# One more half of a gated convolution taken as weighted sums out of PSUM: a memory attention kernel whose order of work is written out as a list

## The chip, the cores and the metric

The kernel runs on one core of a Trainium2 chip. The metric is the device time of one execution in microseconds (us). The engines of the core work from queues of their own, each strictly in the order in which the program gave it instructions: TensorE (PE in the profile, its weight loads PEld) for matrix products, VectorE (DVE), ScalarE (ACT), GpSimd (POOL), and SyncE (SP), which here only issues DMA transfers. An engine waits at the head of its queue until what its next instruction reads has been written, and until the buffer it writes has been given up.

## What is computed

The inputs are `q`, `k`, `v` (8 batches x 8 heads x 576 positions x 64), `phi` (8 x 8 x 576 x 32), a projection `w_val` and `w_out` (512 x 512 each) and `conv_w` (5 x 512). Cut to what matters:

```python
a = exp(phi - max over s);  a = a / sum over s            # per batch, head, slot
k_m, v_m = a.T @ k, a.T @ v                               # 32 slots x 64 per head
p = softmax(q @ k_m.T / 8)                                # s x 32 per head
x = p @ v_m                                               # heads side by side: s x 512
gate = sigmoid(sum over i of conv_w[i] * x shifted by i)  # causal, five taps, per channel
out = (gate * (x @ w_val)) @ w_out
```

## The kernel before, in words

All eight batches run through the same steps. A batch's 576 positions are cut into two **halves** `s` = 0, 1 of 288 columns, and its 512 channels into two **groups** `g` = 0, 1 of four heads each. Values are laid out with channels (or slots) on the 128 partitions and positions along the free axis.

For a batch `b`: `load_phi`, `phi_max`, `phi_turn`, `phi_top`, `phi_spread`, `phi_lay`, `phi_sub`, `phi_exp` make the unnormalised slot weights; `slots` (L397) multiplies them with `k` and `v`; `slots_inv` and `slots_scale` (L404, L406, L416/L418) normalise; `slots_turn` and `slots_place` transpose the result; `scores` (L447) is the product with `q`, in PSUM tiles called `cv`; `scores_turn` (L459), `soft_max`, `soft_sub` (L492), `soft_exp`, `soft_sum`, `soft_inv`, `soft_mul` (L519) and `soft_turn` (L525) are the softmax, whose last step writes the tile `pT` (probabilities, slots on partitions). Each batch needs its `pT` before the two ways to the gate can start.

The pre-activation of the gate is made in one of two ways, half by half:

- `conv(b, s)` (L585): `taps` has multiplied `v_m` with each of the five tap weights; TensorE then accumulates five shifted products per head, 40 matrix products for a half, and `sigmoid` (L632) reads the finished sum from PSUM.
- `mix(b, s)` (L598): 8 matrix products make `x` itself for 292 columns, in PSUM. Then `tap(b, s, g, i)` adds the five taps: i = 0 is a scaled copy on ACT (L620), i = 1 to 4 are multiply-adds on DVE (L622), each of two planes of 288 columns. If the step is marked with a star, tap 4 goes by ACT into a tile `part` of its own and POOL adds it (L614). `open_gate` (L627) is the sigmoid.

`cv` has two PSUM buffers, which `scores`, `conv` and `mix` share; each is given up when the last reader of it is done. Then `value` (L642, six products of two-piece operands, for a quarter of the channels) makes `x @ w_val`; `gated` (L655) multiplies by the gate, on DVE, or after a copy by ACT (L653) on POOL; `gated_high` and `gated_low` (L214, L217) split the product into two pieces; `project` (L675) is 12 products with `w_out`; `place` copies the result to SBUF, `store` writes it out. `value`, `project`, `slots` and all transposes share four PSUM buffers called `b`. At the start the three weights are also converted from 64-bit floating point by `narrow_size` and `narrow_round` on ACT (L273, L286), `narrow_bits` on DVE (L278), `narrow_add` on POOL (L292) and `narrow_done` on DVE (L301). `warm` is a few products whose result nobody reads.

What sets the order is one text, `ORDER`: a list of about 950 step names. A loop at the end of the kernel runs it from front to back, and each step appends its instructions to the queues of its engines. A star at a name makes the step take its other engine (`pick(usual, other)`). So the list fixes the order on each engine's queue and on SP's. In the kernel before, both halves of batch 0 go by `conv` and the other 14 halves by `mix`.

Of the kernel before, what the change touches and what calls it, by code (L numbers as in the profile page):

```python
# [43 lines left out]
warm.8 phi_exp.0.0 narrow_round.v.2 place_taps.0 narrow_bits.v.2 narrow_add.v.2 narrow_done.v.2 slots.0.0
slots_inv.0.0 slots_scale.0.0* narrow_done.v.3 slots.0.1 slots_inv.0.1 load_w.v.1 narrow_size.v.1 spread_taps.1
load_q.0.0 narrow_round.v.1 place_taps.1 load_q.0.1 warm.2 slots_scale.0.1 slots_turn.0 slots_place.0 load_w.o.0
narrow_bits.v.1 narrow_add.v.1 scores.0 narrow_done.v.1 narrow_round.o.0 taps.0.0 scores_turn.0.0 load_w.o.2
narrow_size.o.0 soft_max.0.0 soft_sub.0.0* taps.0.1 narrow_bits.o.0 narrow_size.o.2 narrow_bits.o.2 turn_taps.0
# [5 lines left out]
slots_inv.1.1 slots_scale.1.1* slots_inv.1.0 slots_scale.1.0* narrow_add.o.3 narrow_done.o.3 load_phi.2 conv.0.1
slots_turn.1 phi_max.2 phi_turn.2 soft_low.0.1 value.0.0.1 phi_top.2 narrow_round.o.1 narrow_add.o.1 slots_place.1
sigmoid.0.1.1 sigmoid.0.1.0 phi_spread.2 narrow_done.o.2 phi_lay.2 phi_sub.2 narrow_done.o.1 wo_high.1 wo_low.1
load_q.1 scores.1.0 wo_high.2 gated.0.0.1 scores_turn.1.0 scores.1.1 scores_turn.1.1 val_rows.1 val_copy.1.0
val_copy.1.1 soft_max.1 soft_sub.1 load_phi.3 value.0.1.0 gated.0.1.0 phi_max.3 value.0.0.3 gated.0.0.3 value.0.0.2
gated.0.0.2 value.0.0.0 gated.0.0.0 narrow_done.o.0 value.0.1.1 phi_exp.2 phi_turn.3 phi_top.3 wo_low.2 soft_exp.1
soft_sum.1 val_high.1.0 load_rest.2 value.0.1.3 gated_high.0.0.0 gated_low.0.0.0 load_kv.2.1 slots.2.1 load_kv.2.0  # L60
slots.2.0 slots_inv.2.1 gated.0.1.1 wo_high.3 soft_inv.1* soft_mul.1* soft_turn.1 slots_scale.2.1* gated.0.1.3
gated_high.0.0.1 gated_low.0.0.1 slots_inv.2.0 slots_scale.2.0 phi_spread.3 phi_lay.3 wo_high.0 wo_low.0 wo_low.3
value.0.1.2 warm.2 soft_high.1 load_phi.4 gated.0.1.2 val_low.1.0 phi_max.4 mix.1.1 tap.1.1.1.0* tap.1.1.1.1
tap.1.1.1.2 tap.1.1.1.3 project.0.0.0 slots_turn.2 gated_high.0.1.0 place.0.0.0 gated_high.0.1.1 soft_low.1 load_q.2
gated_low.0.1.0 project.0.0.1 phi_turn.4 slots_place.2 val_rows.2 tap.1.1.0.0 tap.1.1.0.1 load_kv.3.1 tap.1.1.1.4
tap.1.1.0.2 val_high.1.1 val_low.1.1 place.0.0.1 val_copy.2.0 val_high.2.0 scores.2.0 open_gate.1.1.1 scores_turn.2.0
val_low.2.0 val_copy.2.1 project.0.0.3 place.0.0.3 tap.1.1.0.3 tap.1.1.0.4 gated_low.0.1.1 scores.2.1 project.0.0.2
place.0.0.2 scores_turn.2.1 mix.1.0 tap.1.0.0.0 phi_top.4 value.1.1.3 soft_max.2 gated.1.1.3 soft_sub.2 tap.1.0.0.1
tap.1.0.0.2 tap.1.0.1.0* tap.1.0.1.1 project.0.1.0 tap.1.0.1.2 tap.1.0.1.3 phi_sub.3 load_rest.3 tap.1.0.1.4
soft_exp.2 value.1.0.2 store.0.0.1 soft_sum.2 soft_inv.2 soft_mul.2 project.0.1.1 place.0.1.0 place.0.1.1 val_high.2.1  # L70
project.0.1.3 phi_spread.4 tap.1.0.0.3 tap.1.0.0.4 phi_lay.4 phi_exp.3 phi_sub.4 value.1.1.2 place.0.1.3 gated.1.1.2
soft_turn.2 project.0.1.2 open_gate.1.1.0 place.0.1.2 open_gate.1.0.1 slots.3.1 slots_inv.3.1 slots_scale.3.1
load_kv.3.0 slots.3.0 gated_high.1.1.1 slots_inv.3.0 gated_low.1.1.1 slots_scale.3.0 gated.1.0.2 open_gate.1.0.0
mix.2.1 tap.2.1.0.0 value.1.1.1 gated.1.1.1* store.0.0.0 tap.2.1.0.1 tap.2.1.0.2 tap.2.1.0.3 tap.2.1.0.4 value.1.1.0
gated.1.1.0* slots_turn.3 value.1.0.1 slots_place.3 gated.1.0.1* value.1.0.3 gated.1.0.3 gated_high.1.1.0
gated_low.1.1.0 load_kv.4.0 value.1.0.0 gated.1.0.0* tap.2.1.1.0* load_rest.4 val_rows.3 val_low.2.1 val_copy.3.1
load_q.3 scores.3.0 store.0.1.1 load_phi.5 phi_max.5 gated_high.1.0.1 gated_low.1.0.1 project.1.1.1 store.0.1.0
load_kv.4.1 gated_high.1.0.0 gated_low.1.0.0 load_kv.5.0 tap.2.1.1.1 scores_turn.3.0 tap.2.1.1.2 tap.2.1.1.3
project.1.1.0 place.1.1.1 scores.3.1 scores_turn.3.1 val_copy.3.0 project.1.1.3 tap.2.1.1.4 phi_exp.4 soft_max.3
soft_sub.3 place.1.1.3 val_high.3.0 mix.2.0 tap.2.0.0.0 phi_turn.5 project.1.0.1 project.1.1.2 phi_top.5 soft_high.2  # L80
soft_low.2 place.1.1.0* soft_exp.3 tap.2.0.0.1 tap.2.0.0.2 tap.2.0.0.3 soft_sum.3 slots.4.0 slots_inv.4.0 load_rest.5
place.1.1.2 soft_inv.3 soft_mul.3 tap.2.0.1.0* tap.2.0.1.1 load_q.4 tap.2.0.0.4 slots.4.1 tap.2.0.1.2 project.1.0.0
place.1.0.1 val_high.3.1 slots_scale.4.0* soft_turn.3 place.1.0.0 store.1.1.1 store.1.0.0 phi_spread.5 phi_lay.5
# [661 lines left out]
```

## Time and profile before

| | |
|---|---|
| median of 3 runs | 252.11 us (251.46 to 253.62) |
| profiled execution | 251.45 us, of which 249.7 us are the span shown by the profile |
| TensorE busy, mean granted clock | 92% of the span, 0.979 |
| VectorE, ScalarE, GpSimd busy | 82%, 73%, 68% |
| DMA | 47.78 MB, 191 GB/s over the span |
| chain that ended last, by engine | PE 73%, DVE 18%, ACT 2%, POOL 2% |

The 1.75 us between the execution and its span lie around the profile's first and last instruction. A share of busy time is a mean over stages; the profile also gives it stretch by stretch, and that is the table to read beside the chain of waits, which is followed back from the last instruction to whatever released each step.

### The profile page before, as it was taken

Reading aid. Unit: us, or ns where it says so; the run is one execution under the profiler, and the core shown is the slowest. Engines: PE = TensorE matmul, PEld = TensorE weight load, DVE = VectorE, ACT = ScalarE, POOL = GpSimd, SP = SyncE. Lnnn points to the kernel's source line nnn. Section 1 sums busy time; section 2 is a strip of 40 time slices with the busy share of each in tenths; the row PEclk is TensorE's granted clock in tenths of the full one; section 3 lists DMA queues with packets and bytes.
Section 4 is the critical chain, followed back from the end, with each engine's and each line's share of the span. In section 5 each row is a group of like instructions: output and inputs, shape, how many; then the busy total and the mean of one; then the engine's idle time right before and its main releaser. Section 6 shows DMA issues by size and latency. Waiting matters only on the chain.

```text
span 249.7 us, 6632 instructions
## 1 busy us (share of the span) xinstructions
PE 230.2 (92%) x2664; PEld 199.8 (80%) x2664; DVE 205.9 (82%) x413; ACT 182.5 (73%) x350; POOL 171.0 (68%) x128
## 2 busy tenths in 40 slices
...
GB/s 215 418 414 406 410 272 277 217 139 367 15 350 376 398 251 105 257 371 198 31 361 191 50 50 182 131 239 128 112 3 95 3 0 97 174 18 1 142 97 95
DMA packets 12142, 47.78 MB, mean 191 GB/s; under 512 B 1352, under 2 KB 1864, under 8 KB 9168
## 3 DMA queue, kind: packets, MB, share of 16 engines
...
## 4 chain that ended last, share of the span: by engine, by line
PE 73%; DVE 18%; ACT 2%; POOL 2%; issue 2%; DMA 1%; SPq 0%; POOLq 0%; DVEq 0%; ACTq 0%
PE b L675 39%; PE b L642 18%; PE cv L598 4%; PE b L397 3%; PE cv L447 3%; PE b L547 2%; DVE pT L525 2%; DVE st L519 2%; DVE gate L622 2%; DVE mx L343 1%; DVE ss L503 1%; DMA raw<-in_conv_w_dram 1%; PE cv L585 1%; DVE hH L301 1%; DVE st L459 1%
## 5 line engine op out<-in xcount | busy, mean ns | idle before, releaser
L622 DVE SCALAR_TENSOR_TENSOR gate<-cv,cwP,gate 128x288 f32<-128x288 f32 x200 | 87.4, 504 | 3.2 <-ACT gate L620 3.1
L675 PE MATMUL b<-hL,woH 128*128 128x288 f32 x256 | 76.4, 299 | 0.2 <-PE cv L598 0.2
L675 PE MATMUL b<-hH,woL 128*128 128x288 f32 x256 | 76.1, 297 | 0.0
L675 PE MATMUL b<-hH,woH 128*128 128x288 f32 x256 | 75.4, 294 | 0.0
L217 POOL TENSOR_TENSOR hL<-h,hH 128x576 fp32r<-128x576 f32 x31 | 44.8, 1455 | 12.1 <-ACT hH L214 7.0
L675 PEld LDWEIGHTS b<-hL,woH 128*128 128x128 f32 x256 | 48.1, 188 | 5.1 <-issue 2.0
L675 PEld LDWEIGHTS b<-hH,woL 128*128 128x128 f32 x256 | 48.1, 188 | 0.2 <-POOL woL L217 0.2
L675 PEld LDWEIGHTS b<-hH,woH 128*128 128x128 f32 x256 | 48.1, 188 | 0.0
L214 ACT COPY o<-b 128x288 f32<-128x288 f32 x50 | 19.6, 404 | 26.9 <-PE b L675 25.9
L642 PE MATMUL b<-pL,vwH 128*128 128x288 f32 x128 | 29.4, 311 | 0.0
L655 POOL TENSOR_TENSOR h<-h,gate 128x288 f32<-128x288 f32 x20 | 16.0, 809 | 17.6 <-ACT h L653 17.2
L642 PE MATMUL b<-pH,vwL 128*128 128x288 f32 x128 | 27.3, 295 | 0.0
L642 PE MATMUL b<-pH,vwH 128*128 128x288 f32 x128 | 27.3, 294 | 0.0
L655 DVE TENSOR_TENSOR h<-b,gate 128x288 f32<-128x288 f32 x44 | 18.9, 448 | 9.0 <-ACT gate L627 4.3
L620 ACT ACTIVATE gate<-cv,cwP 128x288 f32<-128x288 f32 x56 | 24.8, 506 | 0.4 <-PE cv L598 0.2
L642 PEld LDWEIGHTS b<-pL,vwH 128*128 128x128 f32 x128 | 20.1, 188 | 5.2 <-issue 1.7
L292 POOL TENSOR_TENSOR hH<-hH,hL 128x512 int32<-128x512 int32 (+1 forms) x9 | 12.8, 1424 | 16.4 <-DVE hH L278 9.0
L217 POOL TENSOR_TENSOR vwL<-vwF,vwH 128x512 fp32r<-128x512 f32 x14 | 18.4, 1313 | 8.1 <-ACT vwH L214 4.7
L627 ACT ACTIVATE gate<-gate 128x576 f32<-128x576 f32 x28 | 19.4, 696 | 5.4 <-DVE gate L622 4.5
L397 PE MATMUL b<-kv,e 128*32 128x129 f32 x512 | 19.0, 293 | 2.8 <-ACT e L388 2.7
L397 PEld LDWEIGHTS b<-kv,e 128*32 128x32 f32 x512 | 15.4, 141 | 7.2 <-ACT e L388 4.9
L642 PEld LDWEIGHTS b<-pH,vwL 128*128 128x128 f32 x128 | 20.5, 188 | 0.0
...
## 6 DMA issues: line engine op xcount, KB each, us to landing
...
raw<-in_w_val_dram SPq DMA_DIRECT2D x4, 512.0 KB, 6.7
raw<-in_w_out_dram SPq DMA_DIRECT2D x4, 512.0 KB, 7.8
...
```

Of the source, the lines that this page charges most:

```text
L214: eng.copy(out=out, in_=x) if eng is nc.scalar else eng.tensor_copy(out=out, in_=x)
L217: eng.tensor_tensor(out=out, in0=x, in1=hi.bitcast(F32), op=ALU.subtract)
L292: nc.gpsimd.tensor_tensor(out=a, in0=a, in1=r, op=ALU.add)
L397: nc.tensor.matmul(km[j * M:(j + 1) * M, 0:2 * D + 1], lhsT=e[:, g, j * M:(j + 1) * M, c], rhs=x[:, c, j, :] if c < C - 1 else rests[b % 2 ...
L447: nc.tensor.matmul(sc[t][j * M:(j + 1) * M, c, 0:HALF], lhsT=live["kvT", b][rows, x, j * M:(j + 1) * M], rhs=live["q", b][rows, x, j, :], ...
L598: nc.tensor.matmul(cv[g][x * D:(x + 1) * D, j // 2, 0:PAD + HALF], lhsT=live["kvd", b][rows, G, g], rhs=pTs[b % 2][rows, g, s * HALF:(s + ...
L620: nc.scalar.activation(out=o[:, t], in_=x, func=AF.Identity, scale=w)
L622: nc.vector.scalar_tensor_tensor(out=o[:, t], in0=x, scalar=w, in1=o[:, t], op0=ALU.mult, op1=ALU.add)
L627: nc.scalar.activation(out=gt, in_=gt, func=AF.Sigmoid)
L642: nc.tensor.matmul(vp[:, 0:HALF], lhsT=a[:, t // PG, n:n + P], rhs=p[:, g, s * HALF:(s + 1) * HALF], start=(i == 0), stop=(i == len(parts) ...
L655: eng.tensor_tensor(out=h[:, i], in0=x, in1=gt, op=ALU.mult)
L675: nc.tensor.matmul(ps[:, 0:HALF], lhsT=w[:, t, n * P:(n + 1) * P], rhs=a[:, t % 2], start=(i == 0), stop=(i == len(parts) - 1))
```

## The change

Only the text `ORDER` changes; no function does. Batch 0's second half goes by the other way: `conv.0.1` and its two `sigmoid` steps are gone, and `mix.0.1`, ten `tap.0.1` steps and two `open_gate.0.1` steps are there instead. The stars are set anew (12 `tap` pairs go over `part` before, 8 now, so DVE has 224 multiply-adds in place of 200), and the order of all steps is another one, the transfers on SP among them. Of the diff two lines of each side:

```diff
-load_phi.0.0 phi_max.0.0 phi_turn.0.0 load_phi.0.1 load_w.c.0 narrow_size.c.0 narrow_bits.c.0 phi_max.0.1 phi_turn.0.1
...
-narrow_bits.o.3 conv.0.0 sigmoid.0.0.1 load_kv.1.0 soft_mul.0.1* soft_turn.0.1 slots.1.0 sigmoid.0.0.0 soft_high.0.1
...
+load_w.v.0 narrow_size.v.0 narrow_round.v.0 narrow_bits.v.0 narrow_add.v.0 narrow_done.v.0 load_w.v.3 load_phi.0.1
...
+conv.0.0 sigmoid.0.0.0 narrow_done.o.1 sigmoid.0.0.1 load_kv.1.1 mix.0.1 narrow_done.o.3 slots.1.1 slots_inv.1.1
```

Line numbers of the changed kernel are higher by 2, as its text is two lines longer.

**The opening of VectorE's queue**, before (the first eight instructions after the start; `mx` is the maximum of `phi`, `hH` a weight under conversion, `taps<-raw` the converted `conv_w`):

```order
L343 TENSOR_REDUCE mx<-e 128x128
L278 TENSOR_SCALAR hH<-hH 8x320
L343 TENSOR_REDUCE mx<-e 128x128
L361 TENSOR_REDUCE top<-b 128x1 x2
L383 TENSOR_TENSOR e<-e,b 128x640
L343 TENSOR_REDUCE mx<-e 128x256
L301 SCALAR_TENSOR_TENSOR taps<-raw,hH 8x320
L383 TENSOR_TENSOR e<-e,b 128x640
```

and now:

```order
L280 TENSOR_SCALAR hH<-hH 128x512
L303 SCALAR_TENSOR_TENSOR w_val_sb<-raw,hH 128x512
L280 TENSOR_SCALAR hH<-hH 128x512
L345 TENSOR_REDUCE mx<-e 128x128
L303 SCALAR_TENSOR_TENSOR w_val_sb<-raw,hH 128x512
L280 TENSOR_SCALAR hH<-hH 8x320
L345 TENSOR_REDUCE mx<-e 128x128
L363 TENSOR_REDUCE top<-b 128x1
L303 SCALAR_TENSOR_TENSOR taps<-raw,hH 8x320
```

Two quarters of `w_val` are converted in front of and between the first maxima of `phi`, whose transfers stand behind them on SP's queue too.

**VectorE's queue from the end of batch 0's softmax on**, before (behind the transpose that finishes `pT` of batch 0, the tile `pT_74`; `h<-b,gate` is `gated`, L459 `scores_turn` of batch 1):

```order
L404 TENSOR_SCALAR ri<-b 128x1
L406 RECIPROCAL ri<-ri 128x1
L404 TENSOR_SCALAR ri<-b 128x1
L406 RECIPROCAL ri<-ri 128x1
L301 SCALAR_TENSOR_TENSOR hH<-raw,hH 128x512
L343 TENSOR_REDUCE mx<-e 128x256
L361 TENSOR_REDUCE top<-b 128x2
L301 SCALAR_TENSOR_TENSOR hH<-raw,hH 128x512 x2
L655 TENSOR_TENSOR h<-b,gate 128x288
L459 STREAM_TRANSPOSE st<-cv 128x576 x2
L485 TENSOR_REDUCE mm<-st 128x36
L655 TENSOR_TENSOR h<-b,gate 128x288
```

and now (L624 is the multiply-add of a tap, L461 `scores_turn`):

```order
L219 TENSOR_TENSOR pL<-pT_74,pH 128x2x288
L303 SCALAR_TENSOR_TENSOR hH<-raw,hH 128x512 x2
L406 TENSOR_SCALAR ri<-b 128x1
L408 RECIPROCAL ri<-ri 128x1
L624 SCALAR_TENSOR_TENSOR gate<-cv,cwP,gate 128x288 x10
L461 STREAM_TRANSPOSE st<-cv 128x576
L345 TENSOR_REDUCE mx<-e 128x256
L461 STREAM_TRANSPOSE st<-cv 128x576
L487 TENSOR_REDUCE mm<-st 128x36
L494 TENSOR_TENSOR st<-st,mm 128x1152
```

Ten multiply-adds of batch 0's second half now stand ahead of batch 1's softmax, whose subtraction (L494) is on DVE now. The other four, and a `scores_turn` of batch 2, follow before the transpose of batch 1's `pT_76`:

```order
L505 TENSOR_REDUCE ss<-st 128x36
L514 TENSOR_SCALAR ss<-ss 128x36
L515 RECIPROCAL ss<-ss 128x36
L624 SCALAR_TENSOR_TENSOR gate<-cv,cwP,gate 128x288 x2
L657 TENSOR_TENSOR h<-b,gate 128x288 x2
L624 SCALAR_TENSOR_TENSOR gate<-cv,cwP,gate 128x288 x2
L461 STREAM_TRANSPOSE st<-cv 128x576
L527 STREAM_TRANSPOSE pT_76<-st 128x2x576
L461 STREAM_TRANSPOSE st<-cv 128x576
```

Before, that transpose came after these:

```order
L655 TENSOR_TENSOR h<-b,gate 128x288 x3
L301 SCALAR_TENSOR_TENSOR hH<-raw,hH 128x512
L361 TENSOR_REDUCE top<-b 128x2
L503 TENSOR_REDUCE ss<-st 128x36
L404 TENSOR_SCALAR ri<-b 128x1
L406 RECIPROCAL ri<-ri 128x1
L655 TENSOR_TENSOR h<-b,gate 128x288
L513 RECIPROCAL ss<-ss 128x36
L519 TENSOR_TENSOR st<-st,ss 128x1152
L525 STREAM_TRANSPOSE pT_76<-st 128x2x576
```

The multiply of batch 1's `soft_mul` (L519, 128x1152) has moved to POOL.

**TensorE's queue ahead of the first `mix` of batch 1** (which reads `pT_76`), before:

```order
L397 MATMUL b<-kv_80,e 32x129 x16
L397 MATMUL b<-rest_81,e 32x129 x4
L397 MATMUL b<-kv_79,e 32x129 x16
L397 MATMUL b<-rest_81,e 32x129 x4
L370 MATMUL b<-ident,top 128x128 x2
L642 MATMUL b<-pL,vwH 128x288 x2
L642 MATMUL b<-pH,vwL 128x288 x2
L642 MATMUL b<-pH,vwH 128x288 x2
L224 MATMUL cv<-ident 128x128 x2
L598 MATMUL cv<-pT_76,kvd 64x292 x8
```

and now:

```order
L429 MATMUL b<-ident,kvd 128x128 x3
L449 MATMUL cv<-q,kvT 32x288 x8
L372 MATMUL b<-ident,top 128x128 x2
L549 MATMUL b<-w_val_sb,kvT 32x512 x8
L449 MATMUL cv<-q,kvT 32x288 x8
L644 MATMUL b<-pL,vwH 128x288 x2
L644 MATMUL b<-pH,vwL 128x288 x2
L644 MATMUL b<-pH,vwH 128x288 x2
L600 MATMUL cv<-pT_76,kvd 64x292 x8
```

`slots_turn`, both halves of `scores` and `val_rows` of batch 2 (L429, L449, L549) stand ahead of that `mix` now; before they came behind it.

## Rows read from the trace of the kernel before

**Rows 1.** The page, part 1: busy time of each engine over the whole execution, its share of the span, and instructions.

```profile
PE 230.2 (92%) x2664; PEld 199.8 (80%) x2664; DVE 205.9 (82%) x413; ACT 182.5 (73%) x350; POOL 171.0 (68%) x128
```

**Rows 2.** The view of stretches: first and last microsecond of the stretch, its length, then busy time and number of instructions of each engine, the granted clock of PE, and the DMA engines' share and rate.

```profile
0.00:31.70 31.70, 19.25 (x224) 12.82 (x224) 21.54 (x37) 16.77 (x31) 13.34 (x21) 0.89 0.95 373
31.70:56.20 24.50, 21.97 (x392) 17.64 (x392) 22.45 (x38) 19.34 (x36) 16.46 (x11) 0.94 0.60 223
56.20:140.00 83.80, 83.76 (x1016) 71.61 (x1016) 78.90 (x168) 76.30 (x145) 77.47 (x52) 1.00 0.65 244
233.40:249.70 16.30, 12.70 (x96) 12.46 (x95) 3.92 (x9) 4.12 (x9) 3.33 (x3) 1.00 0.33 122
```

**Rows 3.** The timeline of PE (start, duration, engine, line, operation, tiles, shape, count; idle time before it and what ended it in brackets): the two `conv` of batch 0, and the first `mix` of batch 1.

```profile
31.70 4.21 PE L585 MATMUL cv<-pT,taps 32*64 32x288 f32 x80 [0.28 <-DVE pT L525]
37.79 3.02 PE L585 MATMUL cv<-pT,taps 32*64 32x288 f32 x80 [0.62 <-DVE ri L404]
56.20 0.75 PE L598 MATMUL cv<-pT,kvd 32*64 32x292 f32 x16 [1.28 <-DVE pT L525]
```

**Rows 4.** The view of waits, for DVE up to 56.2 us: who waited for whom, us in total, times, longest. Below it, from the view of DMA issues, two kinds of transfer: how many, KB each, us from issue to landing (the second is half a `phi`).

```profile
DVE w_val_sb L301 <- POOL hH L292: 4.1, 3, 1.5
DVE mx L343 <- DMA e<-in_phi_dram: 3.6, 1, 3.6
DVE top L361 <- PE b L354: 2.0, 2, 1.4
...
raw<-in_w_val_dram SPq DMA_DIRECT2D x4, 512.0 KB, 6.7
e<-in_phi_dram SPq DMA_DIRECT2D x2, 320.0 KB, 3.0
```

**Rows 5.** The chain of waits that ended last, in order of time: start, us, what (rows of PE after 56 us, the taps of one half, and the last stretch of PE).

```profile
59.07 0.33 PE b L427 x3
61.22 1.02 PE b L547 x16
62.23 0.49 PE cv L447 x16
64.50 0.65 PE cv L447 x16
69.19 4.25 DVE gate L622 x10
233.39 12.72 PE b L675 x96
```

**Rows 6.** Groups of instructions by line, engine, operation and shape: count, busy us, mean ns of one, then idle time before them.

```profile
L492 DVE TENSOR_TENSOR st<-st,mm 128x1152 f32<-128x1152 f32 x1 | 1.3, 1347 | 0.0
L492 DVE TENSOR_TENSOR st<-st,mm 128x576 f32<-128x576 f32 x2 | 1.5, 758 | 0.1
L459 DVE STREAM_TRANSPOSE st<-cv 128x576 f32<-128x576 f32 x16 | 12.2, 770 | 1.1 <-PE cv L447 1.0
L655 DVE TENSOR_TENSOR h<-b,gate 128x288 f32<-128x288 f32 x44 | 18.9, 448 | 9.0 <-ACT gate L627 4.3 <-PE b L642 2.9 <-issue 0.8
L512 DVE TENSOR_SCALAR ss<-ss 128x36 f32<-128x36 f32 x5 | 1.2, 232 | 0.1
L404 DVE TENSOR_SCALAR ri<-b 128x1 f32<-128x1 f32 x16 | 2.3, 143 | 0.3 <-PE b L397 0.3
L406 DVE RECIPROCAL ri<-ri 128x1 f32<-128x1 f32 x16 | 2.6, 164 | 0.5
L301 DVE SCALAR_TENSOR_TENSOR taps<-raw,hH 8x320 int32<-8x320 int32 x1 | 0.5, 470 | 0.0
L572 POOL TENSOR_TENSOR taps<-cwB,kvd 128x320 f32<-128x320 f32 x2 | 2.2, 1102 | 0.0
L614 POOL TENSOR_TENSOR gate<-gate,part 128x576 f32<-128x576 f32 x12 | 17.1, 1428 | 2.6 <-DVE gate L622 2.5
L655 POOL TENSOR_TENSOR h<-h,gate 128x288 f32<-128x288 f32 x20 | 16.0, 809 | 17.6 <-ACT h L653 17.2 <-POOL hL L217 0.3
L519 POOL TENSOR_TENSOR st<-st,ss 128x1152 f32<-128x1152 f32 x5 | 10.7, 2145 | 5.9 <-DVE ss L513 4.8 <-ACT o L214 1.1
L620 ACT ACTIVATE gate<-cv,cwP 128x288 f32<-128x288 f32 x56 | 24.8, 506 | 0.4 <-PE cv L598 0.2
L273 ACT ACTIVATE hH<-raw 128x512 f32<-128x512 f32 x8 | 5.4, 676 | 1.5 <-DMA raw<-in_w_out_dram 0.9 <-DMA raw<-in_w_val_dram 0.6
```

**Rows 7.** The timeline of DVE and POOL, four places: the last step of a weight's conversion alone and beside an operation of POOL, the multiply of `soft_mul` alone and beside one, and one `slots_scale` on DVE.

```profile
38.06 0.69 DVE L301 SCALAR_TENSOR_TENSOR hH<-raw,hH 128x512 int32<-128x512 int32 x1
49.04 1.80 DVE L301 SCALAR_TENSOR_TENSOR hH<-raw,hH 128x512 int32<-128x512 int32 x1
48.99 1.30 POOL L217 TENSOR_TENSOR woL<-hH,woH 128x512 fp32r<-128x512 f32 x1
53.37 1.36 DVE L519 TENSOR_TENSOR st<-st,ss 128x1152 f32<-128x1152 f32 x1
180.24 2.47 DVE L519 TENSOR_TENSOR st<-st,ss 128x1152 f32<-128x1152 f32 x1
180.06 1.43 POOL L217 TENSOR_TENSOR hL<-h,hH 128x576 fp32r<-128x576 f32 x1 [0.46 <-DVE hH L214]
80.26 0.54 DVE L418 TENSOR_SCALAR kvd<-b,ri 128x128 f32<-128x128 f32 x2
```

More of the change, by code (lines that the diff above doesn't have):

```diff
@@ L44 @@
[L44 to L48, printed above, removed]
@@ L54 @@
[L54 to L58, printed above, removed]
@@ L59 @@
[L59 to L83, printed above, removed]
@@ new lines @@
+load_kv.0.1 wo_low.0 load_w.v.1 narrow_round.v.1 place_taps.1 slots_inv.0.0 slots_scale.0.0 taps.0.0 slots.0.1
+slots_inv.0.1 slots_scale.0.1 slots_turn.0 load_q.0.0 wo_high.2 narrow_size.v.1 narrow_bits.v.1 narrow_add.v.1
+slots_place.0 load_q.0.1 scores.0 taps.0.1* narrow_done.v.1 load_w.o.3 narrow_round.o.3 narrow_size.o.3 wo_low.2
+scores_turn.0.0 scores_turn.0.1 soft_max.0.0 narrow_bits.o.3 phi_exp.1 soft_max.0.1 val_rows.0 val_copy.0.0
+soft_sub.0.0 soft_exp.0.0 load_phi.2 phi_max.2 soft_sub.0.1 soft_exp.0.1 warm.2 soft_sum.0.0 soft_inv.0.0
@@ new lines @@
+slots.2.1 slots_inv.2.1 slots_scale.2.1* value.0.1.0 value.0.1.1 value.0.1.3 open_gate.0.1.0 slots_turn.2
+slots_place.2 soft_sum.1 soft_inv.1 tap.0.1.1.3 gated_high.0.0.1 wo_low.1 gated.0.1.1 load_q.2 scores.2.0 gated.0.1.0
+tap.0.1.1.4 scores_turn.2.0 gated_high.0.1.0 val_high.1.1 phi_spread.3 soft_mul.1 phi_lay.3 load_rest.3
+open_gate.0.1.1 val_rows.2 val_copy.2.0 scores.2.1 soft_turn.1 scores_turn.2.1 soft_high.1 value.0.1.2 mix.1.1
+gated.0.1.3 gated.0.1.2 tap.1.1.1.0 wo_low.3 gated_low.0.0.1 project.0.0.1 val_low.1.1 soft_max.2 tap.1.1.1.1
```

167 lines of the change are left out of this document (97 added, 70 removed).

## The prediction, made before the changed kernel ran

> **What bounds the kernel now.** I first read the busy shares [rows 1]: TensorE 92%, VectorE 82%, ScalarE 73%, GpSimd 68%. A mean over the span says little, so next comes the table of stretches [rows 2]. Up to 31.7 us no engine is near its limit. From 31.7 to 56.2 us VectorE is the busiest (22.45 of 24.5 us). From 56.2 to 140 us TensorE is never idle (83.76 of 83.8), with the three others at 91 to 94%. In the last 16.3 us only TensorE has work to speak of. Two views say where the border lies. The timeline of TensorE [rows 3] shows the first `mix` of batch 1 starting at 56.20 after 1.28 us of idleness, released by VectorE's transpose that writes `pT`; the second `conv` also waited, 0.62 us, for VectorE. The chain of waits [rows 5] runs over TensorE from there on almost without a break, and its last piece, 12.72 us of `project` from 233.39, ends at 246.11.
>
> So there are two regimes. Until 56.2 us VectorE's queue decides when batch 1's `pT` is ready; it holds 21.54 + 22.45 = 44.0 us of work in 56.2 [rows 2], so 12.2 us of idleness. Its named waits are 3.6 us for the first `phi`, 4.1 us for POOL's adds in the weights' conversion and 2.0 us for TensorE's transposes [rows 4]; 2.5 us remain in smaller ones. After 56.2 us the time is the sum of TensorE's work. The sum below therefore asks two things: how much later does that `mix` start, and how much of TensorE's work is left by then?
>
> **VectorE's work ahead of that `mix`.** Compared by the order, what stands ahead of batch 1's `soft_turn` differs so:
> - 14 multiply-adds of `tap.0.1` are new (8 for one group, 6 for the starred one). Ten in a row took 4.25 us [rows 5], so 0.425 each: +5.95.
> - Batch 1's `soft_sub` comes over from POOL, +1.35; the two half-size ones of batch 0 leave, -2 x 0.758 = -1.52 [rows 6].
> - Batch 1's `soft_mul` leaves for POOL: -1.36 [rows 7].
> - A `scores_turn` of batch 2 moves ahead, +0.77, and its `slots_inv.2.0`, +0.143 + 0.164 = +0.31; three `gated` go to POOL, -3 x 0.448 = -1.34; the add of `soft_inv.1` comes from ACT, +0.23 [rows 6].
> - `slots_scale.0.0` comes from ACT, +0.54 [rows 7].
> - `taps.0.1` comes from POOL. No row shows it on VectorE. The nearest, a VectorE operation on as many elements on 8 partitions, takes 0.47, and on POOL it took 1.10 [rows 6]; 0.47 is the same engine, so I take that.
>
> Together +5.40 us.
>
> **VectorE's idleness ahead of it.** The new queue begins with a weight. A quarter of `w_val` is 512 KB against 320 KB for half a `phi` [rows 4]; 192 KB at the stretch's 373 GB/s [rows 2] is 0.5 us, and `narrow_size` on ACT (0.68 [rows 6]) comes in between: +1.2. Waits for POOL's adds were three for 4.1 us; I count four places now where the last step of a conversion comes right behind the step that feeds the add: +1.4. The two waits for transposes (2.0) go, since conversion steps stand between `phi_max` and `phi_top`. Of the unnamed 2.5 us I take 1.5 as filled in the same way. Net -0.9. This is the softest term. Its bounds: +2.6, if neither kind of filling happens (1.2 + 1.4); -5.0, if the waits for POOL are filled too (-0.9 - 4.1).
>
> **TensorE.** `conv.0.1` (3.02 [rows 3]) becomes a `mix` (0.75), so 2.27 us of its work go. But that work lies ahead of the `mix` of batch 1, in the regime in which TensorE waits for VectorE; I count it at nothing. Its cover is the wait for `pT`. What counts is what is left behind that `mix`: `slots_turn`, `scores` and `val_rows` of batch 2 now run ahead of it, 0.33 + 0.49 + 0.65 + 1.02 = -2.49 [rows 5]. One new wait: `scores.2.1` holds a `cv` buffer until its `scores_turn`, which stands right behind the transpose on VectorE (0.77 [rows 6]). The second group of the `mix` needs that buffer; the first group's products (half of 0.75) cover part of it: +0.4. Queued behind it are `project.0.0` and all of TensorE.
>
> **The other engines.** ACT gets six plane scalings (0.51 each [rows 6]) and three copies ahead of that point, and loses two sigmoids of similar length to the two new ones; it idles 5.2 us between 31.7 and 56.2 [rows 2]. POOL gets `soft_mul.1` (2.15), three `gated` (0.81 each) and the add of `part` (1.43) [rows 6], some 6 us, and gives up batch 1's `soft_sub`, `taps.0.1`; it idles 8.0 us there [rows 2]. I cost both at nothing; if that cover is gone, POOL's multiply of `soft_mul.1` is late next, and `pT` with it. Behind 56.2 us VectorE's total hardly changes: ten further multiply-adds (+4.25) stand against a second `soft_mul` (2.47 beside POOL [rows 7]) and some copies that leave. That `soft_mul` (batch 6) was on the chain; on POOL it takes 2.15 [rows 6]: -0.3.
>
> **Neighbours.** The last step of a conversion takes 0.69 us alone and 1.80 beside POOL's subtraction that began at 48.99, a difference of 1.11, and the multiply 1.36 alone and 2.47 beside one that began at 180.06, again 1.11 [rows 7]. I cost such meetings at no change, as the start held some before; one more or fewer on the queue is worth 1.1.
> The Trainium skill, Perfetto Trace Analysis, section Optimizing Scalar/DVE Operations, says that GpSimd and VectorE share a read port, so that moving operations from one to the other might not help. By that rule the 4.22 us that leave for POOL here (1.52, 1.36, 1.34) would come back as longer neighbours, and the sum would be 257.8; the trace agrees only for those neighbours that were lengthened, by 1.11 each.
>
> **Sum.** +5.40 - 0.9 + 0.4 - 2.49 - 0.3 = +2.1 us. The profiled execution took 251.45, so **253.6 us**. That execution lies 0.66 below the median of the runs shown; against the median, 253.6 is +0.6%, within the 1% that a measurement of this kernel can just tell from no change (249.6 to 254.6).
>
> **Rivals.**
> - *TensorE is the bound all along* (249.2 us). Then the 2.27 us saved come straight off 251.45. For it: 92% busy [rows 1], and no idleness from 56.2 to 140 [rows 2]. Against it: the 1.28 us wait right where the saved work would count [rows 3]. It decides if batch 1's first `mix` starts by about 56 us. The Trainium skill, Perfetto Trace Analysis, section Identifying the Most-Contended Engine, would have one optimise the engine with the highest occupancy first, judging TensorE by its weight loads; they are 80% here [rows 1], and the trace agrees only from 56 us on. Chance 0.12.
> - *The start swallows the taps* (249.5 us, or in part, up to the forecast). The waits for POOL's adds are filled too: 253.6 - 4.1. For it: 12.2 us of idleness stand against 5.4 of new work. Against it: an engine that works strictly in order can't fill a wait with what stands behind it. Chance 0.20.
> - *Slower* (257.0 us). Past 56 us all four engines are at 91% or more [rows 2], and each `mix` needs both `cv` buffers, so it waits for the last tap of the half before. VectorE, 5 us late, doesn't catch up, and the `mix` waits for one more pair of multiply-adds (0.85) at four places: +3.4 on the forecast. It decides if the 14 taps of `tap.1.1` (5.95 us) end later than four `project` behind the first `mix` (12.72 / 8 = 1.59 each [rows 5]) and one `slots`; that is close. Chance 0.22.
>
> That the change doesn't do what it says is no case here: the order shows one `conv` and 224 multiply-adds.
>
> **Chances and range.** The forecast has 0.46; its soft term and one meeting more or less give it 251.3 to 256.0. Faster by over 1%: most of the first rival and half of the second, 0.18. Slower by over 1%: nearly all of the third and a third of the forecast, 0.35. Within 1%: 0.47. The range for 8 in 10 reaches to the rivals, 249.3 to 257.1.
>
> **What would show it.** In the changed profile: TensorE's first `mix` of batch 1 at about 60 to 61 us instead of 56.2, released by VectorE; VectorE's busy time up to it about 49 us; TensorE's idleness ahead of it longer, by some 3 to 4 us; from it to the end of TensorE's last product 187 us instead of 189.9, with no more idleness than before; VectorE's first instruction at 4.8 us. A first `mix` by 57 us, or TensorE waiting at later `mix` steps, would make it wrong, in the one direction or the other.

## The result, and the profile after

The changed kernel takes 253.22 us (median of 20 runs, 252.23 to 258.22) against 251.75 us for the kernel before in the same comparison (20 runs, 251.41 to 253.62): a ratio of 1.0068, 95% interval 1.0052 to 1.0085. It is 0.7% slower, inside the 1% that I had called no change. The profiled execution of the changed kernel took 252.53 us (span 250.5), that of before 251.45; the difference of the two is 1.08 us, and all that is counted out below is counted against that. One run each of the changed kernel (258.22 us), of e8 (259.14) and of e13 (257.74) counts as slow, being over 1.5% above the fastest of its kernel, and is left out of the ratios, of the medians and ranges of e8 and e13, and of the spread at the end.

Page, part 1, of the changed kernel (answers to [rows 1]):

```profile
PE 228.0 (91%) x2600; PEld 196.6 (78%) x2600; DVE 210.0 (84%) x433; ACT 180.5 (72%) x347; POOL 175.2 (70%) x130
```

TensorE has 2.2 us less to do, VectorE 4.1 us more. Shares alone say nothing about which of the two counts. The table of stretches does, cut where batch 1's first `mix` now starts, at 60.6 us ([rows 2] has it cut at 56.2):

```profile
31.70:56.20 24.50, 20.23 (x367) 15.06 (x365) 24.05 (x45) 22.50 (x45) 16.98 (x13) 1.00 0.86 331
0.00:60.60 60.60, 41.50 (x601) 28.00 (x601) 48.75 (x90) 42.66 (x79) 38.06 (x39) 1.00 0.90 344
60.60:140.00 79.40, 79.39 (x940) 69.24 (x941) 74.34 (x157) 72.39 (x141) 73.10 (x47) 1.00 0.60 227
140.00:247.30 107.30, 107.13 (x1061) 99.39 (x1060) 86.92 (x188) 65.07 (x129) 64.03 (x46) 1.00 0.22 78
```

Two lines of the same view of the kernel before, for comparison:

```profile
0.00:56.20 56.20, 41.22 (x615) 30.46 (x615) 44.00 (x74) 36.11 (x66) 29.81 (x32) 0.91 0.80 308
140.00:246.20 106.20, 105.25 (x1042) 97.68 (x1034) 83.04 (x173) 69.77 (x141) 63.69 (x46) 1.00 0.25 92
```

VectorE (third busy time in a row) now works 48.75 us before that `mix`, 24.05 of 24.5 in the stretch from 31.7 us. Behind it TensorE idles 0.01 and 0.17 us. So there are still two regimes, with the border 4.4 us later. One thing changed besides: TensorE's granted clock up to the border was 0.91 and is 1.00 now: the first `conv` ran at 0.64 and took 4.21 us before [rows 3], and takes 2.69 now. What this is worth in the time, no run shows. The timeline of TensorE (answers to [rows 3]) shows the border, and the only `conv` that is left:

```profile
35.63 2.69 PE L587 MATMUL cv<-pT,taps 32*64 32x288 f32 x80 [1.16 <-DVE pT L527]
39.04 1.26 PE L600 MATMUL cv<-pT,kvd 32*64 32x292 f32 x16 [0.73 <-DVE ri L406]
60.61 1.39 PE L600 MATMUL cv<-pT,kvd 32*64 32x292 f32 x16 [0.18 <-DVE pT L527]
```

The `mix` at 60.61 still waits for the transpose `pT`, though only 0.18 us: batch 2's `scores` and `val_rows` fill TensorE's time ahead of it. It takes 1.39 us instead of 0.75, since its second group needs the `cv` buffer that batch 2's second `scores` holds until VectorE's transpose of it ends, at 61.23. The last piece of the chain of waits (answers to [rows 5]) ends at 229.65 + 17.61 = 247.26:

```profile
42.27 4.24 DVE gate L624 x10
60.61 1.39 PE cv L600 x16
229.65 17.61 PE b L677 x132
```

From the first `mix` to that end it is 247.26 - 60.61 = 186.65 us; before, it was 246.11 - 56.20 = 189.91 [rows 3, 5]. So the change loses 60.61 - 56.20 = 4.41 us ahead of the `mix` and gains 3.26 behind it: +1.15, against 1.08 measured.

**Where the 4.41 us come from.** VectorE's busy time ahead of the `mix` went from 44.0 to 48.75 (+4.75), its idleness from 12.2 to 60.6 - 48.75 = 11.85 (-0.35). The waits of VectorE up to 60.6 us (answers to [rows 4]):

```profile
DVE hH L280 <- ACT hH L275: 5.0, 1, 5.0
DVE w_val_sb L303 <- POOL hH L294: 3.3, 3, 1.5
DVE hH L303 <- POOL hH L294: 1.6, 1, 1.6
DVE ri L406 <- PE b L399: 1.2, 1, 1.2
```

Four waits for POOL's adds, 4.9 us in place of 4.1; the first instruction at 5.0 in place of 3.6; the two waits for transposes (2.0) are gone, but one of 1.2 for the second `slots` of batch 0 is new.

**Where the 3.26 us come from.** TensorE's groups behind the first `mix`, first of the kernel before (from 56.2 us), then of the changed one (from 60.6): products and busy us of `slots_turn`, `scores`, `val_rows` and `mix`.

```profile
L427 PE MATMUL b<-ident,kvd 128*128 128x128 f32 x18 | 3.0, 274 | 0.0
L447 PE MATMUL cv<-q,kvT 64*32 64x288 f32 x192 | 8.0, 407 | 0.0
L547 PE MATMUL b<-w_val_sb,kvT 64*32 64x512 f32 x96 | 6.5, 599 | 0.0
L598 PE MATMUL cv<-pT,kvd 32*64 32x292 f32 x224 | 10.5, 430 | 2.0 <-DVE pT L525 1.3 <-DVE ri L404 0.7
```

```profile
L429 PE MATMUL b<-ident,kvd 128*128 128x128 f32 x15 | 2.5, 272 | 0.0
L449 PE MATMUL cv<-q,kvT 64*32 64x288 f32 x160 | 6.2, 408 | 0.0
L549 PE MATMUL b<-w_val_sb,kvT 64*32 64x512 f32 x80 | 5.4, 599 | 0.0
L600 PE MATMUL cv<-pT,kvd 32*64 32x292 f32 x224 | 11.1, 430 | 0.2 <-DVE pT L527 0.2
```

One batch's share of the first three kinds (3, 32 and 16 products) has left: 0.5 + 1.8 + 1.1 = 3.4 us, summed over groups whose products overlap in part; the `mix` rows grew by 0.6. By stretches, where overlap counts once, TensorE's busy time behind the border was 83.76 + 105.25 = 189.01 us and is 79.39 + 107.13 = 186.52, thus 2.5 less, with the longer `mix` in it. The rest is idleness: 0.04 us up to 140 and 0.95 behind it before, 0.18 in all now, thus 0.8 less. Nearly all of that is one place of the kernel before:

```profile
184.18 0.75 PE L598 MATMUL cv<-pT,kvd 32*64 32x292 f32 x16 [0.68 <-DVE ri L404]
```

This `mix` of batch 6 waited for VectorE, where the multiply of 2.47 us [rows 7] and the transpose behind it ended at 184.12, and the first `project` behind the `mix` waited 0.16 more. With the multiply on POOL both waits are gone.

### The profile page after: what moved, and what is told of

It reads as the page before. It is cut to its first block, busy times and chain, and to the rows that moved or that the text cites. A ratio compares the mean times of both kernels' runs of the same rounds, so it can differ in the third digit from the quotient of the medians.

```text
span 250.5 us, 6520 instructions
## 1 busy us (share of the span) xinstructions
PE 228.0 (91%) x2600; PEld 196.6 (78%) x2600; DVE 210.0 (84%) x433; ACT 180.5 (72%) x347; POOL 175.2 (70%) x130
## 4 chain that ended last, share of the span: by engine, by line
PE 73%; DVE 18%; POOL 4%; DMA 1%; ACT 1%; issue 1%; DVEq 0%; POOLq 0%
PE b L677 39%; PE b L644 18%; PE b L399 7%; PE cv L600 4%; DVE gate L624 3%; PE cv L449 2%; PE b L549 2%; POOL hH L294 2%; DVE mx L345 2%; DVE pT L527 2%; DVE ss L505 2%; DMA raw<-in_w_val_dram 1%; DVE st L461 1%; DVE mm L487 1%; DVE w_val_sb L303 1%
## 5 line engine op out<-in xcount | busy, mean ns | idle before, releaser
L624 DVE SCALAR_TENSOR_TENSOR gate<-cv,cwP,gate 128x288 f32<-128x288 f32 x224 | 98.3, 506 | 2.7 <-ACT gate L622 2.4
L219 POOL TENSOR_TENSOR hL<-h,hH 128x576 fp32r<-128x576 f32 x29 | 42.8, 1484 | 4.1 <-ACT hH L216 3.7
L216 ACT COPY o<-b 128x288 f32<-128x288 f32 x53 | 20.9, 404 | 28.0 <-PE b L677 18.7
L657 POOL TENSOR_TENSOR h<-h,gate 128x288 f32<-128x288 f32 x23 | 18.4, 808 | 27.7 <-ACT h L655 13.8
L622 ACT ACTIVATE gate<-cv,cwP 128x288 f32<-128x288 f32 x60 | 26.4, 505 | 7.7 <-PE cv L600 7.7
L629 ACT ACTIVATE gate<-gate 128x576 f32<-128x576 f32 x30 | 20.5, 687 | 3.9 <-DVE gate L624 3.9
L657 DVE TENSOR_TENSOR h<-b,gate 128x288 f32<-128x288 f32 x41 | 17.7, 446 | 6.0 <-PE b L644 3.4
L216 ACT CAST hH<-h 128x576 fp32r<-128x576 f32 x28 | 18.9, 681 | 3.8 <-DVE h L657 3.0
L219 POOL TENSOR_TENSOR vwL<-vwF,vwH 128x512 fp32r<-128x512 f32 x15 | 19.4, 1295 | 3.1 <-ACT vwH L216 3.1
L294 POOL TENSOR_TENSOR hH<-hH,hL 128x512 int32<-128x512 int32 (+1 forms) x9 | 11.5, 1283 | 14.0 <-DVE hH L280 9.7
```

Of the source, the lines that this page charges most:

```text
L216: eng.copy(out=out, in_=x) if eng is nc.scalar else eng.tensor_copy(out=out, in_=x)
L219: eng.tensor_tensor(out=out, in0=x, in1=hi.bitcast(F32), op=ALU.subtract)
L294: nc.gpsimd.tensor_tensor(out=a, in0=a, in1=r, op=ALU.add)
L622: nc.scalar.activation(out=o[:, t], in_=x, func=AF.Identity, scale=w)
L624: nc.vector.scalar_tensor_tensor(out=o[:, t], in0=x, scalar=w, in1=o[:, t], op0=ALU.mult, op1=ALU.add)
L629: nc.scalar.activation(out=gt, in_=gt, func=AF.Sigmoid)
```

## The experiments

Twelve kernels. My theory: VectorE's queue sets when batch 1's first `mix` starts, and TensorE alone the 187 us behind it. The rivals: TensorE bounds all of it; the start has room for the taps; VectorE bounds the later part too. To read every run the same way I use two numbers of its trace: the start of that `mix`, and the time from there to the end of TensorE's last product. The trace is that of one execution, whose own time stands beside the median; the two differ by up to 1.8 us.

| run | median us (runs) | traced execution | first `mix` | from it to the end |
|---|---|---|---|---|
| before | 251.75 (20) | 251.45 | 56.20 | 189.9 |
| changed | 253.22 (20) | 252.53 | 60.61 | 186.6 |
| e1 | 257.67 (4) | 258.69 | 63.41 | 189.9 |
| e2 | 254.0 (6) | 253.97 | 62.05 | 186.8 |
| e3 | 256.17 (4) | 256.35 | 63.84 | 187.2 |
| e4 | 255.68 (4) | 255.96 | 62.68 | 187.9 |
| e5 | 257.77 (4) | 256.7 | 64.77 | 186.7 |
| e6 | 254.6 (4) | 255.39 | 61.62 | 188.7 |
| e7 | 252.78 (12) | 253.37 | 60.75 | 187.3 |
| e8 | 255.71 (3) | 255.71 | 63.32 | 187.3 |
| e10 | 257.47 (4) | 258.77 | 65.29 | 188.3 |
| e12 | 254.41 (4) | 253.93 | 60.77 | 187.8 |
| e13 | 254.34 (5) | 254.81 | 62.74 | 186.9 |
| e14 | 255.04 (6) | 256.88 | 64.30 | 187.4 |

**e1: the taps alone, in the order of before.**

```diff
 (before, order of steps)
-conv.0.1
+mix.0.1
-sigmoid.0.1.1 sigmoid.0.1.0
+tap.0.1.0.0* tap.0.1.0.1 ... tap.0.1.1.4 open_gate.0.1.0 open_gate.0.1.1
```

> The order of the kernel before, with only batch 0's second half taken out of PSUM: mix in the place of conv, ten taps and two gates in the place of its two sigmoids; nothing else moves. Theory (VectorE's queue sets when batch 1's first mix starts, TensorE's work sets the rest): 14 multiply-adds of 0.425 us go into that queue, nothing leaves it, and no TensorE work is moved ahead: first mix at 62 us instead of 56.2, time 251.8 + 5.9 = 257.7 us (256.5 to 258.5). Rival 'TensorE is the bound all along': 2.3 us of conv saved, 249.5 us. Rival 'the start's idleness swallows the taps': 251.8 to 254 us.

Measured: 257.67 us (257.36 to 258.69), ratio 1.024 [1.020, 1.028]. The theory's number. TensorE saves the `conv`, yet the first `mix` starts 7.2 us later, and TensorE's waits say for whom:

```profile
PE cv L448 <- DVE gate L623: 4.4, 2, 2.3
```

```profile
45.65 1.22 PE L448 MATMUL cv<-q,kvT 64*32 64x288 f32 x16 [2.28 <-DVE gate L623]
48.94 1.22 PE L448 MATMUL cv<-q,kvT 64*32 64x288 f32 x16 [2.07 <-DVE gate L623]
```

Batch 1's `scores` wait for the `cv` buffers that VectorE's taps hold. Both rivals fall here: the time is 6 us longer and not shorter, and the start swallows nothing. But the 7.2 us are 1.4 more than the 5.8 forecast, and the taps need not be all of them: TensorE's granted clock was 0.68 from 31.7 to 56.2 us, against 0.94 before [rows 2], so that 16 products of the `scores` took as long as 32 did before (1.22 us, at 42.45). How much of the 1.4 us this explains stays open. What e1 shows all the same is that the new order, not the new way of convolving, holds the time near that of before: it takes back 257.67 - 253.22 = 4.45 us.

**e3: VectorE 2.7 us longer ahead of the first `mix`.**

```diff
 (changed kernel; a spare reduction over st, its result unused, 1.35 us each)
 soft_max.1
+spare.1 spare.1
```

> The changed kernel with two more reductions on VectorE (1.35 us each, their result is read by nobody), right behind batch 1's soft_max, ahead of its first mix. Theory: every microsecond on VectorE there moves the first mix: +2.7, time 255.9 us. Rival 'TensorE is the bound all along': 253.2 us. Rival 'the start's idleness swallows it': under 254.5 us.

Measured: 256.17 us (255.09 to 256.35), ratio 1.0165 [1.0125, 1.0205]: 2.95 above the changed kernel, and the first `mix` is 3.23 later, 0.5 more than was added (TensorE's granted clock was 0.66 from 55 to 60 us there, 1.00 in the changed kernel). Ahead of that `mix` VectorE's work counts in full.

**e4 and e12: the same late, behind the last taps, and in the middle.**

```diff
 (changed kernel)
 tap.7.0.1.4
+spare.7 spare.7
```

> The same two reductions, placed behind the last tap of batch 7's first half, where TensorE has the work of several projects queued. Theory: hidden, 253.2 us (up to 253.7). If VectorE's total set the time, +2.7 as in the early place: 255.9 us.

Measured: 255.68 us (253.52 to 256.47), ratio 1.014 [1.0083, 1.0198]. A miss, for two reasons. The `mix` came at 62.68, 2.07 us later than in the changed kernel, though nothing ahead of it was changed (more on this below). And 187.9 us behind it are 1.3 more than 186.6: at that place the spares kept `gated` waiting, and TensorE waited for it:

```profile
PE b L682 <- DVE h L662: 1.0, 1, 1.0
```

So I put one behind batch 4's `soft_max` and one behind batch 6's.

```diff
 (changed kernel)
 soft_max.4
+spare.4
 soft_max.6
+spare.6
```

> The changed kernel with one spare reduction of 1.35 us on VectorE behind soft_max of batch 4 (about 106 us) and one behind soft_max of batch 6 (about 168 us); their results are not used. Theory (behind the first mix TensorE alone sets the time, VectorE has slack): from the first mix of batch 1 to the last product 186.7 to 187.4 us, time 252.7 to 253.9 us. Rival (VectorE, near 94% busy there, is on the path as well): 188 to 189.4 us, time 254.5 to 256 us.

Measured: 254.41 us (253.93 to 254.88), ratio 1.0103 [1.0075, 1.0131], 187.8 us behind the `mix`: between the two theories. Of 2.7 us some 1.2 count. "TensorE alone sets the time behind the first `mix`" is too simple: where VectorE is 91 to 94% busy, under half of what is added to it comes through, without one long wait (0.4 us of named waits on TensorE).

**e5 and e6: the two halves of the orders exchanged.**

```diff
 (e5: before up to mix.1.1, then the changed kernel's order)
 ... phi_max.4
+slots_turn.2 slots_place.2 load_q.2 scores.2.0 scores_turn.2.0 ... val_rows.2 val_copy.2.0 scores.2.1 scores_turn.2.1
 mix.1.1
 (e6: the changed kernel up to mix.1.1, then the order of before)
```

> Up to the first mix of batch 1 this is the order of before (conv for both halves of batch 0); behind it, the steps that are left in the order of the change, which begins with batch 2's slots_turn, scores and val_rows. Theory (the loss is made ahead of that mix, and the order behind it is the better one): the mix starts at 57 to 58.5 us, being 56.2 plus what of the 2.49 us of batch 2's work does not fit into the 1.28 us of idleness there; 186.7 us from it to the last product as in the changed kernel; time 249 to 251 us. Rival (the order behind the mix runs without idleness only because it starts late): TensorE waits behind the mix, 251.5 to 253.5 us.

Measured: 257.77 us (256.7 to 259.63), ratio 1.0262 [1.0217, 1.0308]. Missed by 7 us: the first `mix` starts at 64.77 where 57 to 58.5 was forecast. TensorE's timeline, and SyncE's queue that loads `q`:

```profile
57.23 0.75 PE L428 MATMUL b<-ident,kvd 128*128 128x128 f32 x3 [2.35 <-DVE kvd L419]
61.46 1.22 PE L448 MATMUL cv<-q,kvT 64*32 64x288 f32 x16 [3.48 <-DMA q<-in_q_dram]
```

```profile
52.63 0.33 SPq L235 DMA_DIRECT2D e<-in_phi_dram  x1
53.01 0.89 SPq L250 DMA_DIRECT2D q<-in_q_dram  x1
```

Batch 2's `q` stands behind a `phi` on SyncE's queue and is issued at 53.01, in the changed kernel at 48.06; the `scores` moved ahead without it wait 3.48 us, and the `mix` behind them too. Another 2.35 us go to the scaled slots, which VectorE makes only behind `pT`, and TensorE's granted clock was 0.66 from 56 to 66 us: `val_rows` took 1.97 us there, 1.32 in the changed kernel. I had costed the moved products and not what they wait for. The 186.7 us behind the `mix` are the theory's.

> Up to the first mix of batch 1 this is the order of the change (taps for the second half of batch 0, batch 2's steps ahead); behind it, the steps that are left in the order of before. Theory (the start sets it): first mix at 60.6 us or somewhat later, then about 187 us; time 253 to 254.5 us. Rival (the new order behind the mix is worth something by itself): 255 us or more. Rival (it is the new order behind the mix that costs): 251 us or less.

Measured: 254.6 us (254.34 to 255.39), ratio 1.0117 [1.0093, 1.0141]. Between the theory (up to 254.5) and the first rival (from 255): the `mix` at 61.62, then 188.7 us, 2.1 more than with the new order behind it. The new order is thus worth something there too. TensorE is idle for 1.3 us behind the `mix`, where it is 0.2 in the changed kernel; the two longest waits are 0.42 for a `gate` of VectorE at 70.88 and 0.70 at batch 6's `mix`, the place named above, since the old order has its multiply on VectorE again:

```profile
188.21 0.75 PE L600 MATMUL cv<-pT,kvd 32*64 32x292 f32 x16 [0.70 <-DVE ri L406]
```

The other 0.9 us are longer busy time, which I did not place.

**e2, e10 and e13: `conv` back in the new order.** The half's two sigmoids take the place of its taps. In e2 they stand where the `mix` and the taps stood, in e10 behind batch 1's `val_rows`, in e13 behind batch 1's second `slots`.

```diff
 (changed kernel)
-mix.0.1
-tap.0.1.0.0* ... tap.0.1.1.4 open_gate.0.1.0 open_gate.0.1.1
 (e2) load_kv.1.1
+conv.0.1
 (e10) scores.1.0 val_rows.1
+conv.0.1 sigmoid.0.1.0 sigmoid.0.1.1
 (e13) slots.1.1 slots_inv.1.1 lay_taps.0 phi_spread.2 phi_lay.2
+conv.0.1
```

> The changed kernel's order, with batch 0's second half given back to conv: conv in the place of mix, two sigmoids in the place of the first taps, the other taps and the two gates gone. Theory: 14 multiply-adds (5.9 us) leave VectorE's queue ahead of batch 1's first mix; conv's 3 us may show in part, as the next slots and the scores of batch 1 stand behind it on TensorE. First mix at 55 to 59 us instead of 60.6, time 247.5 to 251.5 us, faster than the changed kernel's 253.2. Rival 'TensorE is the bound all along': 2.3 us more work, 255.5 us.

Measured: 254.0 us (253.59 to 254.82), ratio 1.0088 [1.0054, 1.0123]; a miss. VectorE lost 6 us of taps and gained 5.3 of waits for TensorE:

```profile
44.09 0.16 DVE L405 TENSOR_SCALAR ri<-b 128x1 f32<-128x1 f32 x1 [1.57 <-PE b L398]
48.19 0.78 DVE L460 STREAM_TRANSPOSE st<-cv 128x576 f32<-128x576 f32 x1 [3.75 <-PE cv L448]
```

Batch 1's `slots` and `scores` stand behind the `conv` on TensorE, and VectorE needs them. Up to the `mix` VectorE works 43.04 us (48.75 in the changed kernel) and idles 19.0 (11.85); 0.49 us of that is a late transfer, of the kind told at the end. So in the new order the `conv`'s time is on the path, while in the old one saving it bought nothing (e1). Could it stand elsewhere?

> The changed kernel with conv and two sigmoids for the second half of batch 0 in place of its mix and taps, as in the earlier run of that kind, but the conv behind batch 1's scores and val_rows instead of ahead of its slots. Theory (there the conv's 3 us on TensorE lay on the path to VectorE's transposes, 5.3 us of waits): VectorE's waits of 1.57 and 3.75 us shrink to under 2 in all, the first mix of batch 1 starts at 56.5 to 59 us, the time is 248.5 to 251.5 us. Rival (TensorE has no room for a conv anywhere ahead of that mix): first mix at 61 to 62 us, 253 to 254.5 us.

Measured: 257.47 us (256.43 to 258.77), ratio 1.0228 [1.0188, 1.0268]: the worst of the three. VectorE's waits for the `scores` are 2.90 and 0.65 us, and a new one of 1.93 is for ACT's exponentials of batch 1: ACT does the `conv`'s sigmoids ahead of them and loads a function table ahead of the sigmoids and another ahead of the exponentials (1.28 us each, at 51.96 and 56.83).

> The changed kernel with conv and two sigmoids for the second half of batch 0, as in the two earlier runs of that kind, but the conv directly behind batch 1's second slots and phi_spread of batch 2, the sigmoids behind the copy of batch 1's kvT. Theory (in the first of those runs VectorE's 5.3 us of waits came from the conv standing ahead of those slots, and the slots were late in turn for the scores): the slots are ready some 3 us earlier, the conv runs while kvT is being made, the waits fall to 2 to 3.5 us, the first mix of batch 1 starts at 59 to 60.5 us (with the landing of w_out as in the changed kernel's profile), time 251.5 to 253 us. Rival (TensorE's work ahead of the scores counts wherever it stands): first mix at 61.5 us or later, 253.5 to 254.5 us.

Measured: 254.34 us (253.66 to 256.05), ratio 1.0104 [1.0073, 1.0135], `mix` at 62.74: the rival's number. But the trace shows two reasons that the rival does not name. The `slots` did come earlier, and then the last steps of two conversions (VectorE, line 302) met POOL's subtraction; e13 first, then its POOL, then e2:

```profile
40.24 3.54 DVE L302 SCALAR_TENSOR_TENSOR hH<-raw,hH 128x512 int32<-128x512 int32 x2
44.08 0.57 ACT L417 ACTIVATE kvd<-b,ri 128x128 f32<-128x128 f32 x2 [3.77 <-DVE ri L407]
```

```profile
39.92 2.72 POOL L384 TENSOR_TENSOR e<-e,mxa 128x1280 f32<-128x1280 f32 x1 [0.21 <-ACT mxa L215]
```

```profile
41.23 1.28 DVE L302 SCALAR_TENSOR_TENSOR hH<-raw,hH 128x512 int32<-128x512 int32 x2
44.86 2.47 POOL L384 TENSOR_TENSOR e<-e,mxa 128x1280 f32<-128x1280 f32 x1 [4.17 <-ACT mxa L215]
```

Alone the two took 1.28 us, in e13 3.54. They were not lengthened alike; the view of that line gives the shortest, median and longest in ns, then the first and last start:

```profile
L302 DVE SCALAR_TENSOR_TENSOR hH<-raw,hH x2: 678/1806/2934, 40.2 to 43.1; 128x512 int32<-128x512 int32 x2
```

The first began at 40.24, when POOL's subtraction had 2.40 us to go (to 42.64), and took 2.93 us, 2.26 longer than alone; the second took 0.68. So a meeting costs about what is left of POOL's operation. [rows 7] reads the same way: both operations there began with 1.25 us of POOL's to go and grew by 1.11. In e2 the late `slots` had kept POOL's subtraction waiting until 44.86. In e13 ACT waited 3.77 us to scale batch 1's slots, and with that most of what was gained ahead was gone. e10 shows the same 3.54. The second reason: batch 2's second `slots` ran at a granted clock of 0.50 (52.89 to 54.86 us), 1.97 us for 32 products instead of 1.06, and VectorE waited 1.80 us for them. The Trainium skill, Perfetto Trace Analysis, section Optimizing Scalar/DVE Operations, says that GpSimd and VectorE share an SBUF read port; here the trace agrees. Taps, which read one operand from PSUM, were not lengthened: in the changed kernel ten of them ran at 0.43 each (42.18 us on, 4.32 in all) while POOL's same subtraction ran from 42.42 to 44.88.

**e8: a weight's conversion later.**

```diff
 (changed kernel)
-narrow_size.o.0 ... narrow_bits.o.0 ... narrow_done.o.0 ... wo_high.0 ... wo_low.0
 slots_inv.0.1
+narrow_size.o.0 narrow_bits.o.0 narrow_round.o.0 narrow_add.o.0
 ...
 narrow_done.v.1
+narrow_done.o.0 wo_high.0 wo_low.0
```

> The changed kernel with the conversion of the first quarter of w_out moved from ahead of batch 0's phi_sub to behind its slots. Theory (the landing of that quarter and POOL's add behind it hold up the whole start, by 0 to 2 us from run to run): the wait of 1.61 us for that add goes, the first mix of batch 1 starts at 59 to 60 us, the time is 250.9 to 252.2 us and its spread over the runs is less than that of the changed kernel (252.2 to 258.2). Rival (the wait only moves to another conversion): 252.9 to 253.5 us with the same spread.

Measured: 255.71 us (254.83 to 256.02), ratio 1.0148 [1.0117, 1.0179]; a miss on the time, and three runs are too few to judge the spread. The wait for the add went (1.61 to 0.32), but batch 0's `slots` came only 0.5 us earlier (18.14 for 18.64), for they wait for ACT's `e`. Then a new wait arose behind them:

```profile
36.98 4.27 PE L587 MATMUL cv<-pT,taps 32*64 32x288 f32 x80 [2.75 <-DVE pT L527]
```

```profile
37.00:41.30 4.30, 4.26 (x80) 2.49 (x80) 4.23 (x10) 2.15 (x3) 2.60 (x2) 0.62 0.56 230
```

TensorE idled 2.75 us ahead of the `conv` (1.16 in the changed kernel), and the `conv` then ran at a granted clock of 0.62, that is for most of the time at the lower level of 1.2 GHz: 4.27 us instead of 2.69. It started 1.35 us later than in the changed kernel and took 1.58 longer; the first `mix` of batch 1 is 2.71 later.

**e7 and e14: idle products ahead of batch 0's `slots`.** In the changed kernel both `slots` of batch 0 took 1.96 us for 32 products, and 1.05 to 1.1 later. The "half the clock" of the expectation is read from these times; the granted clock in the trace is 1.00 there.

```diff
 (changed kernel; e14: the same in e13)
 phi_turn.1
+warm.2
 phi_spread.1
+warm.3
```

> The changed kernel with idle products on TensorE (warm.2 behind batch 1's phi_turn, warm.3 behind its phi_spread), where it idled 1.0 and 1.7 us ahead of batch 0's slots. Theory (in the changed kernel both slots of batch 0 run at half the clock, 1.96 us for 32 products against 1.05 to 1.1 elsewhere, and VectorE waits 1.20 us for the second): one or both take 1.1 to 1.5 us, that wait shrinks by 0.8 to 1.2, the first mix of batch 1 starts at 59.3 to 60 us where the landing of w_out is as in the changed kernel's profile, and the time is 251.5 to 252.7 us. Rival (the wait is taken over by POOL's add of the next conversion): 253 to 253.6 us, first mix at 60.5 us or later.

Measured: 252.78 us (251.28 to 254.58, 12 runs), ratio 1.0034 [1.0008, 1.006]. That is 0.4 below the changed kernel, but the two intervals overlap, and the trace doesn't settle it: the second `slots` took 1.52 us, and in e3, which has no such products, 1.33. Inconclusive.

> The same with the idle products on TensorE ahead of batch 0's slots (warm.2 and warm.3) as in the earlier run. Theory (the two gains lie one behind the other on the path and add up): 0.3 to 0.7 us below the run without them, 251 to 252.6 us. To beat the kernel before by more than the measurement's uncertainty it would have to come below 251 us. Rival (the waits behind take up the gain): the same as without them.

Measured: 255.04 us (254.07 to 256.88), ratio 1.013 [1.0103, 1.0158], not below e13. No version beat the kernel before.

## Why the prediction was right, point by point

The forecast was 253.6, the median is 253.22; the mechanism held, with two regimes and the border at 60.6 us. That the numbers lie so close is in part luck. The sum said +2.1 us on the profiled execution of before, and the profiled executions differ by 1.08. The part ahead of the `mix` came out right (+4.5 forecast, +4.41 measured) with errors that cancel, the gain behind it was larger (-2.4 forecast, -3.26 measured), and the changed kernel's profiled execution lies 0.7 below its median, that of before 0.3 below its own.

- **VectorE's work ahead of the `mix`**: forecast +5.40, measured +4.75. The 14 taps took 6.1 us (5.95 forecast). A part of the difference lies in the meetings with POOL, which I had costed at no change and which went both ways: the last step of four `w_out` conversions took 3.8 us before and 2.6 now, VectorE's eight first steps on the weights 4.3 and 3.2, against +0.9 for one subtraction of `pL` (0.75, now 1.66) and +1.0 for the add of `soft_inv.1` (1.21 beside POOL where I had 0.23). With the smaller ones that is about -0.3; the rest is not placed. The price of 1.1 us per meeting was wrong as well: it is what is left of POOL's operation, 2.26 in e13.
- **VectorE's idleness**: forecast -0.9, measured -0.35. The start came at 5.0 (4.8 forecast), four waits for POOL's adds as counted (but +0.8, not +1.4), the transposes' 2.0 went; what I missed is the new wait of 1.2 for `slots`.
- **The `cv` wait**: forecast 0.4; the `mix` took 0.64 longer.
- **Batch 2's work moved ahead**: forecast -2.49, and -0.3 for the multiply of batch 6. Measured -3.26 in all with the longer `mix` in it. The busy time moved was larger (2.5 + 0.64 = 3.1 by stretches), and the multiply's move to POOL ended 0.84 us of waits at batch 6's `mix`.
- **"I count it at nothing"**, of the saved `conv`: nearly right for the order of before (e1), not for the new one. Even before, the chain of waits runs over that `conv` (37.79, 3.02 us), as VectorE waited 1.39 us at 41.54 for a transpose of `phi` queued behind it; the forecast has that wait under the transposes' 2.0. In the new order the `conv` in place of the taps gives 254.0 (e2), so TensorE's time ahead of batch 1's `scores` is on the path together with VectorE's. The cover I named, the wait for `pT`, had shrunk to 0.18 us.
- **The rivals**: TensorE was not the bound all along and the start did not swallow the taps (e1: +6 us). The slower case, with `mix` waiting at four places, did not come: TensorE names 0.2 us of waits behind 60.6. That TensorE alone sets the time there is too simple all the same (e12). And the weight loads that the first rival cites do not speak for it: at 80% they lie below VectorE's 82% [rows 1].
- **What would show it**: first `mix` at 60 to 61 (60.61), VectorE about 49 (48.75), 187 us to the end (186.65), first instruction at 4.8 (5.0). TensorE's idleness ahead: 56.20 - 41.22 = 14.98 before (41.22 is the same view's busy time up to 56.20), 60.60 - 41.50 = 19.1 now, +4.1 where I had 3 to 4.
